# Attention and two layers of experts: the gates computed behind the first block and stored as lines, pieces of weights measured later, the last scatters unordered and in half rows

## The chip, the cores and the metric

The kernel runs on one core of one Trainium2 chip. The metric is the device time of one execution in microseconds (us). The core has TensorE (PE, multiplications into PSUM), VectorE (DVE), ScalarE (ACT), GpSimd (POOL, which also issues indirect DMAs) and SyncE (SP, which here issues most other DMAs), and 16 DMA engines between memory and SBUF.

## What is computed

Attention over 2 x 8 heads of 768 positions and 64 values, with a window of 16 and summaries of blocks of 32, gives 1,536 rows of 512 values. They pass through two layers of eight experts. In the first each row goes to the one expert with the largest logit; in the second each row goes to all experts, and their results are mixed.

```python
logits = x @ w_gate
expert_idx = np.argmax(logits, axis=1)
probs = softmax(logits)                                   # first layer
out[mask] = probs[arange, expert_idx][mask, None] * (relu(x[mask] @ w1[e]) @ w2[e])
...
P = np.exp(x @ w_gate - max)                              # second layer
for _ in range(8): P /= P.sum(1); P /= P.sum(0); P *= N / E
out += P[:, e:e + 1] * (relu(x @ w1[e]) @ w2[e])          # for all e
```

## The kernel before

The attention writes its result as columns into `xT`; `finished` makes the logits `lg` of two tiles of 128 rows; `rows_out` (L534) turns a tile back and stores it as rows in DRAM, `xd`. The copies `xn` that it stores from have three buffers. Routing (`experts`, `ranks`, `by_lane` and what follows, L379 to L672) sorts the rows by expert into blocks of 256 places: `row_i` says which row stands at a place, `seat_i` where its result goes. 100 filler multiplications (`warm`, L174) follow on PE.

The first layer of experts then runs block by block (`compute`). `fetch(n)` gathers the rows of block n from `xd` with two indirect DMAs on POOL (L1034), and loads its weights, eight pieces of 512 KB, through four buffers `kx` on SP's queue (L152 for w1, L958 for w2). Each piece is split by ACT (`wh`, L944) and DVE (`wl`, L946) into a high and a low part. `turn_rows` transposes the rows (L1066) and splits them (`xh` L1071, `xl` L1072). Layer 1 (L979) makes `hh` and `hl` of 8 column groups, layer 2 (L1001) the results `py`, which are squared, scaled and scattered to `yd` (L1114). For block 0 the w1 pieces are loaded ahead, on a guess of the expert; a branch that every engine takes (L1126, L1127) loads them again if the guess was wrong.

Beside the blocks stands other work, a list of steps called `more`. It is woven from lists with a start each, and one step of it is done at every other call of `step()` inside a block; blocks 1 to 5 take `each` steps apiece. In it are: `gate_square` and `gate_rate` (the size of the second layer's gate weights); `gates` (the exponential and sums that give the first layer's gate of each row), and `gates_out`, which stores them in DRAM, `gd`; and `plain(i, p)` for eight pieces of the second layer's first expert: load into one of three buffers `raw`, square and sum on ACT (`measure`, L740), a rate from it, then the high and low parts. Piece i starts at step 4 i, and piece i + 3 takes the same buffer. The code's order is not the last word: a scheduler places each instruction on its engine by its priorities and by when its operands can be there, and `tc.issue_after(x)` holds an instruction behind x. Thus `gate_square`, `gates` and `gates_out` stood far ahead of block 1, in the routing, since nothing held them there.

The gates are read back as `gated`, by an indirect gather on `gd` (L850), between the two layers.

The second layer takes the largest part of the time. It works by a plan of ticks (`at(tick, f)`), written out by hand: `first` and `second` are its two products, `mixing` gives the functions of the mixing weights, one per tick of a list. `acc` holds the results of all rows in SBUF. In `second`, for the last expert, DVE adds the last parts of two tiles of rows, h = 0 whole at i = 4 and h = 1 by halves at i = 5 (columns 256 on) and i = 6 (columns up to 256), in the order of `SECOND`, 0, 1, 3, 2, 5, 4, 6. Behind i = 4 and i = 6 the tile is scattered to `out` by an indirect DMA on POOL (L1486), twelve in all. All write the same tensor, so each waits for the one before it.

Of the kernel before, what the change touches and what calls it, by code (L numbers as in the profile page):

```python
# [23 lines left out]
P = 128  # L24
NT = B * S
# [83 lines left out]
def body(ctx: ExitStack, tc: tile.TileContext, q, k, v, wg1, w1a, w2a, wg2, w1b, w2b, cst, out):  # L109
# [26 lines left out]
    gex = const.tile([P, NTB, E], F32, name="gex")  # L136
    gse = const.tile([P, NTB], F32, name="gse")
    nblk_i = const.tile([1, 1], I32, name="nblk_i")
    eblk_i = const.tile([1, NBLK], I32, name="eblk_i")
# [878 lines left out]
    if True:  # L1018
# [117 lines left out]
        def gate_square():  # L1136
            sq = wq.tile([P, KC * E], F32, name="wgsq")
            nc.scalar.activation(sq, wg2_sb, AF.Square, accum_out=wgq)
            nc.gpsimd.tensor_copy(wgqb, wgq)
# [6 lines left out]
        def plain(i, p):  # L1146
            idle = lambda: None
            raw = raws[i % 3]
            junk = raw[:, 4:6].rearrange("p a f -> p (a f)").bitcast(BF16)
            return [lambda: p.load(raw), idle, idle, lambda: p.measure(junk), p.measured, p.rate, lambda: (p.raw_hi(), p.sums(fast=True)), lambda: (p.raw_lo(), p.sum4(fast=True)),  # L1150
                    idle, p.sum_hi, p.sum_lo]

        def gates():
            sh = [P, NTB, E]
            nc.vector.tensor_tensor(out=gex, in0=lg, in1=mx.unsqueeze(2).to_broadcast(sh), op=ALU.subtract)
            nc.scalar.activation(gex, gex, AF.Exp)
            nc.vector.tensor_reduce(out=gse, in_=gex, axis=AX.X, op=ALU.add)
            nc.vector.tensor_scalar(gse, gse, 1e-9, None, op0=ALU.add)
            nc.vector.reciprocal(gse, gse)
            nc.vector.tensor_tensor(out=gex, in0=gex, in1=oh, op=ALU.mult)  # L1160
            nc.vector.tensor_reduce(out=gate, in_=gex, axis=AX.X, op=ALU.add)
            nc.vector.tensor_tensor(out=gate, in0=gate, in1=gse, op=ALU.mult)

        def gates_out():
            nc.sync.dma_start(out=gd.rearrange("(t p) o -> p (t o)", p=P), in_=gate)

        more = weave(
            [(0, [gate_square, gate_rate]), (2, [gates, lambda: None, gates_out])]
            + [(4 * i, plain(i, p)) for i, p in enumerate(p2 + p1)]
            + [(4 * (2 * F2 - 1) + 6, [level])]  # L1170
        )
# [92 lines left out]
    def mixing():  # L1264
# [5 lines left out]
        def start1():  # L1270
# [5 lines left out]
            nc.vector.tensor_reduce(out=st[0], in_=lg2, axis=AX.XY, op=ALU.max)  # L1276

        def start2():
            pmt = pz.tile([1, P], F32, tag="m", name="pmt")
            nc.tensor.transpose(pmt, st[0], ident)  # L1280
            st.append(g2.tile([1, 1], F32, tag="gm", name="gm", bufs=1))
            nc.vector.tensor_reduce(out=st[1], in_=pmt, axis=AX.X, op=ALU.max, negate=True)
# [31 lines left out]

        return [start1, start2, start3] + [turn1, turn2, turn3] * 8 + [end]

# [118 lines left out]
    def second(e, k, s, i):  # L1435
# [45 lines left out]
        if i in (2, 4) or e == E - 1:  # L1481
            nc.vector.scalar_tensor_tensor(out=to, in0=p, scalar=w, in1=to, op0=ALU.mult, op1=ALU.add)  # L1482
            if i == 4 and e < E - 1:
                nc.gpsimd.dma_start(out=to, in_=gs[0], accum_op=ALU.add)  # L1484
            if e == E - 1 and i in (4, 6):
                nc.gpsimd.indirect_dma_start(  # L1486
                    out=out, out_offset=bass.IndirectOffsetOnAxis(ap=token_i[:, t : t + 1], axis=0), in_=acc[:, t], in_offset=None,
                    bounds_check=NT - 1, oob_is_err=True,
                )
            return  # L1490
        if i in (0, 5):
# [19 lines left out]
    turns = [66 + 6 * i + t for i in range(8) for t in (0, 2, 4)]  # L1511
    for tick, f in zip([55, 58, 62] + turns + [115], mix):
        at(tick, f)
# [110 lines left out]
```

## Time and profile before

| | us |
|---|---|
| median of 3 runs | 1250.6 |
| lowest and highest | 1245.0, 1256.08 |
| the profiled execution | 1249.01 |
| its span in the profile | 1247.2 |

Mean granted clock of PE over the span: 0.984 (1.00 is 2.4 GHz). Busy shares: PE 95%, DVE 78%, ACT 68%, POOL 21%. Times in the trace are counted from the span's start. A row of the timeline gives start, duration, engine, line, operation and tiles, the count of merged instructions, and in brackets how long its engine stood idle before it and what ended that. Lines are those of the kernel before.

### The profile page before, as it was taken

The numbers are of one execution on the slowest core, as the hardware profiler recorded it, in microseconds if no ns is written. First come the engines' busy times: TensorE is split into PE (matmuls) and PEld (weight loads), VectorE is DVE, ScalarE is ACT, GpSimd is POOL, SyncE is SP. The second block draws the span as 40 slices with busy tenths as digits, with TensorE's granted clock in tenths as the row PEclk, the third lists the DMA queues.
The fourth block names the chain that finished last, engine by engine and source line by source line (L and its number), as shares of the span: only waits on it lengthen the run. The fifth ranks groups of instructions, "written<-read, shape, count | busy, mean of one in ns | idle before, by whom it ended". The sixth has DMA issues, their size and how long they took to land. (4 is left out here: it accounts for less than half of the span.)

```text
span 1247.2 us, 27484 instructions
## 1 busy us (share of the span) xinstructions
PE 1181.1 (95%) x10473; PEld 1044.1 (84%) x10473; DVE 972.6 (78%) x1950; ACT 846.0 (68%) x1595; POOL 265.9 (21%) x331
## 2 busy tenths in 40 slices
PE   6898799999889999999999999999999999999997
PEld 5776688888778788888888888888888888888886
DVE  6695578884588898897878788788978878796763
ACT  5585467774677767776877677677767767776440
POOL 4351212312221220120121112111211211121011
PEclk9899799999999999999999999999999999999999
DMA  9947687862335543665556566555656655663201
GB/s 206 205 97 206 155 275 257 253 208 96 112 111 157 140 130 96 161 148 142 131 119 141 145 162 146 144 115 122 156 137 161 138 135 126 138 149 94 68 35 52
DMA packets 186496, 179.79 MB, mean 144 GB/s; under 512 B 35872, under 2 KB 159520, under 8 KB 185968
## 3 DMA queue, kind: packets, MB, share of 16 engines
q1 hardware_dynamic: 159648, 136.41, 38.6%
q0 software_dynamic: 26704, 41.50, 17.9%
q8 instruction: 85, 1.39, 0.5%
q14 instruction: 59, 0.48, 0.1%
HBM read 131.38 MB, written 15.53 MB: 118 GB/s over the span
## 5 line engine op out<-in xcount | busy, mean ns | idle before, releaser
L1365 PEld LDWEIGHTS <-w1h 128*128 128x128 f16 x2688 | 258.3, 98 | 46.0 <-issue 15.9
L1451 PEld LDWEIGHTS <-hh 128*128 128x128 f16 x2688 | 263.4, 98 | 32.0 <-issue 1.2
L1365 PE MATMUL fx<-kx,w1h 128*128 128x256 f16 x1472 | 257.3, 272 | 8.2 <-ACT c L1372 4.6
L1451 PE MATMUL gx<-w2l,hh 128*128 128x256 f16 x768 | 209.3, 273 | 1.1 <-DVE w2l L780 1.1
L1451 PE MATMUL gx<-w2h,hh 128*128 128x256 f16 x768 | 209.3, 273 | 1.0 <-DVE acc L1482 1.0
L1451 PE MATMUL gx<-w2h,hl 128*128 128x256 f16 x768 | 209.3, 273 | 0.0
L1365 PE MATMUL fx<-kx,w1l 128*128 128x256 f16 x736 | 200.5, 272 | 0.0
L1365 PE MATMUL fa<-kx,w1h 128*128 128x256 f16 x1104 | 193.7, 273 | 0.7 <-ACT yb L1113 0.7
L1372 ACT ACTIVATE c<-fx,kap 128x256 f32<-128x256 f32 x288 | 134.5, 473 | 79.3 <-PE fx L1365 78.8
L1451 PE MATMUL ga<-w2h,hh 128*128 128x256 f16 x576 | 157.6, 274 | 0.0
L1451 PE MATMUL ga<-w2l,hh 128*128 128x256 f16 x576 | 157.6, 274 | 0.0
L1451 PE MATMUL ga<-w2h,hl 128*128 128x256 f16 x576 | 157.5, 273 | 0.0
L1365 PE MATMUL fa<-kx,w1l 128*128 128x256 f16 x552 | 150.7, 273 | 0.0
L1365 PEld LDWEIGHTS <-w1l 128*128 128x128 f16 x1344 | 131.4, 98 | 17.2 <-issue 1.8
L1451 PEld LDWEIGHTS <-hl 128*128 128x128 f16 x1344 | 131.7, 98 | 16.7 <-issue 1.3
L1420 DVE TENSOR_TENSOR hl<-c,hh 128x1024 f16<-128x1024 f32 x96 | 117.1, 1220 | 26.4 <-ACT hh L1417 25.7
L1417 ACT CAST hh<-c 128x1024 f16<-128x1024 f32 x96 | 99.8, 1040 | 34.6 <-DVE c L1414 34.2
L1493 ACT ACTIVATE y<-gx,pws 128x256 f32<-128x256 f32 x144 | 68.2, 474 | 79.9 <-PE gx L1451 62.2
L753 POOL DMA_DIRECT2D raw<-raw x77 | 77.1, 1031 | 210.3 <-DVE w2l L780 97.4
L1375 DVE SCALAR_TENSOR_TENSOR c<-fa,kap,c 128x512 f32<-128x512 f32 x96 | 71.7, 747 | 46.3 <-PE fa L1365 39.9
L1408 DVE SCALAR_TENSOR_TENSOR hl<-c,hh 128x768 f16<-128x768 f32 x96 | 91.2, 950 | 15.4 <-ACT hh L1405 15.4
L1484 POOL DMA_DIRECT2D acc<-y x36 | 31.4, 871 | 336.8 <-ACT c L1372 265.9
(263 smaller groups left out, 2438.6 us busy)
## 6 DMA issues: line engine op xcount, KB each, us to landing
raw<-in_moe_w SPq DMA_DIRECT2D x228, 128.0 KB, 3.5
kx<-in_moe_w SPq DMA_DIRECT2D x56, 512.0 KB, 5.0
kx<-xohd SPq DMA_DIRECT2D x147, 128.0 KB, 3.3
kx<-xold SPq DMA_DIRECT2D x147, 128.0 KB, 3.1
acc<-y POOLq DMA_DIRECT2D x72, 256.0 KB, 4.5
raw<-raw POOLq DMA_DIRECT2D x77, 128.0 KB, 3.6
raw<-in_moe_w SPq DMA_DIRECT2D x38, 256.0 KB, 3.6
vt<-in_v SPq DMA_DIRECT2D x16, 240.0 KB, 7.5
```

Of the source, the lines that this page charges most:

```text
L753: nc.gpsimd.dma_start(out=self.raw[:, to], in_=self.raw[:, of], accum_op=ALU.add)
L1365: nc.tensor.matmul(p, l[:, a, kc * P : (kc + 1) * P], r[:, j, kc], start=new and kc == 0 and m == 0, stop=kc == K2 - 1 and m == 2, skip_gr ...
L1372: nc.scalar.activation(c[:, q], p, f, scale=k_)
L1375: nc.vector.scalar_tensor_tensor(out=c[:, q], in0=x, scalar=k_, in1=c[:, q], op0=ALU.mult, op1=ALU.add)
L1408: nc.vector.scalar_tensor_tensor(out=h[1][:, :3], in0=raw, scalar=0.0, in1=h[0][:, :3], op0=ALU.max, op1=ALU.subtract)
L1417: nc.scalar.copy(h[0][:, 3:], c)
L1420: nc.vector.tensor_tensor(out=h[1][:, 3:], in0=c, in1=h[0][:, 3:], op=ALU.subtract)
L1451: nc.tensor.matmul(p, l, r, start=new and f == 0 and m == 0, stop=f == F2 - 1 and m == 2, skip_group_check=True)
L1484: nc.gpsimd.dma_start(out=to, in_=gs[0], accum_op=ALU.add)
L1493: nc.scalar.activation(gs[h][:, d], p, AF.Copy, scale=w)
```

## The change

It has three parts. First, `gate_square` and `gates` are held behind the layer 1 that was issued last when they are called (`taken[-1]`, which is block 0's or block 1's), `gates` a step later in the list, and `gates_out` turns the gates by a transpose on PE into 12 lines of 128 values and stores those. Second, in `plain` two more idle steps stand between a piece's load and its measurement, and `level` moves by two; the list `more` grows from 39 to 41 steps, and `each` from 8 to 9. Third, for the last expert h = 1 of a pair of tiles is scattered in two half rows, behind i = 5 and i = 6, through a view of `out` with twice as many rows and indices `half_i`; and the scatters are declared free of order among each other.

```diff
+    gt = const.tile([NTB, P], F32, name="gt")
+    half_i = const.tile([P, HTB, 2], U32, name="half_i")
...
-            nc.scalar.activation(sq, wg2_sb, AF.Square, accum_out=wgq)
+            with tc.issue_after(taken[-1][0].ins):
+                nc.scalar.activation(sq, wg2_sb, AF.Square, accum_out=wgq)
...
-            return [lambda: p.load(raw), idle, idle, lambda: p.measure(junk), p.measured, p.rate, lambda: (p.raw_hi(), p.sums(fast=True)), lambda: (p.raw_lo(), p.sum4(fast=True)),
+            return [lambda: p.load(raw), idle, idle, idle, idle, lambda: p.measure(junk), p.measured, p.rate, lambda: (p.raw_hi(), p.sums(fast=True)), lambda: (p.raw_lo(), p.sum4(fast=True)),
                     idle, p.sum_hi, p.sum_lo]
...
-            nc.vector.tensor_tensor(out=gex, in0=lg, in1=mx.unsqueeze(2).to_broadcast(sh), op=ALU.subtract)
+            with tc.issue_after(taken[-1][1].ins):
+                nc.vector.tensor_tensor(out=gex, in0=lg, in1=mx.unsqueeze(2).to_broadcast(sh), op=ALU.subtract)
...
-            nc.sync.dma_start(out=gd.rearrange("(t p) o -> p (t o)", p=P), in_=gate)
+            pt = ps_m.tile([NTB, P], F32, tag="m", name="pt")
+            nc.tensor.transpose(pt, gate, ident)
+            nc.scalar.copy(gt, pt)
+            nc.sync.dma_start(out=gd.rearrange("(t p) o -> t (p o)", p=P), in_=gt)
...
-            [(0, [gate_square, gate_rate]), (2, [gates, lambda: None, gates_out])]
+            [(0, [gate_square, gate_rate]), (3, [gates, lambda: None, gates_out])]
             + [(4 * i, plain(i, p)) for i, p in enumerate(p2 + p1)]
-            + [(4 * (2 * F2 - 1) + 6, [level])]
+            + [(4 * (2 * F2 - 1) + 8, [level])]
...
+        def halves():
+            for h in range(2):
+                nc.vector.tensor_scalar(half_i[:, :, h], token_i[:, HTB:], 2, h, op0=ALU.mult, op1=ALU.add)
...
-            if e == E - 1 and i in (4, 6):
-                nc.gpsimd.indirect_dma_start(
-                    out=out, out_offset=bass.IndirectOffsetOnAxis(ap=token_i[:, t : t + 1], axis=0), in_=acc[:, t], in_offset=None,
-                    bounds_check=NT - 1, oob_is_err=True,
+            if e == E - 1 and i in (4, 5, 6):
+                if i == 4:
+                    to, at_, rows, n = out, token_i[:, t : t + 1], acc[:, t], NT
+                else:
+                    to, at_ = out.rearrange("t (h d) -> (t h) d", h=2), half_i[:, t - HTB, 6 - i : 7 - i]
+                    rows, n = acc[:, t, d], 2 * NT
+                put = nc.gpsimd.indirect_dma_start(
+                    out=to, out_offset=bass.IndirectOffsetOnAxis(ap=at_, axis=0), in_=rows, in_offset=None,
+                    bounds_check=n - 1, oob_is_err=True,
                 )
+                tc.declare_no_dep(put.ins, group="rows", reason="disjoint rows")
+                tc.add_to_no_dep_group("rows", put.ins)
...
-    for tick, f in zip([55, 58, 62] + turns + [115], mix):
+    for tick, f in zip([55, 58, 62] + turns + [115, 118], mix):
```

The order on SP, at the end of the routing, before the change (`raw` are pieces of the second layer, `xn` the rows, `gate` the gates, `eblk_i` the block's expert):

```order
L167 DMA raw_93<-in_moe_w 128x256
L534 DMA xd<-xn 128x512 x3
L1165 DMA gd<-gate 128x12x1
L534 DMA xd<-xn 128x512 x3
L1045 TENSOR_LOAD eblk_i
```

and of the change:

```order
L167 DMA raw_94<-in_moe_w 128x2x256
L168 DMA raw_94<-in_moe_w 128x256
L169 DMA raw_94<-in_moe_w 128x256
L167 DMA raw_95<-in_moe_w 128x2x256
L168 DMA raw_95<-in_moe_w 128x256
L169 DMA raw_95<-in_moe_w 128x256
L536 DMA xd<-xn 128x512 x6
L1047 TENSOR_LOAD eblk_i
```

The store of the gates has left its place between the third and the fourth store of rows; it now stands, as `gd<-gt 12x128`, among the loads of block 2's weights.

The order on ACT, from the routing's last copies to block 0's first relu, before the change (`wgsq` is `gate_square`, `raw,ssq` a measurement):

```order
L533 COPY xn<-pr 128x512 x2
L1156 ACTIVATE gex<-gex 128x96
L533 COPY xn<-pr 128x512 x4
L740 ACTIVATE raw_91,ssq_1730<-raw_91 128x1024
L1138 ACTIVATE wgsq,wgq<-wg_sb 128x32
L740 ACTIVATE raw_92,ssq_1730<-raw_92 128x1024
L740 ACTIVATE raw_93,ssq_1730<-raw_93 128x1024
L1126 TENSOR_LOAD eblk_i
L1127 COMPARE_AND_BRANCH
L1127 UNCONDITIONAL_BRANCH x2
L944 CAST wh_1763<-kx 128x1024
L944 CAST wh_1765<-kx 128x1024
```

and of the change:

```order
L535 COPY xn<-pr 128x512 x6
L742 ACTIVATE raw_93,ssq_1732<-raw_93 128x1024
L742 ACTIVATE raw_94,ssq_1732<-raw_94 128x1024
L742 ACTIVATE raw_95,ssq_1732<-raw_95 128x1024
L1128 TENSOR_LOAD eblk_i
L1129 COMPARE_AND_BRANCH
L1129 UNCONDITIONAL_BRANCH x2
L946 CAST wh_1765<-kx 128x1024
L946 CAST wh_1767<-kx 128x1024
```

`gate_square` and the gates' exponential have left this stretch; the first stands in block 0's layer 2 now, the second in block 1's layer 1.

The order on POOL at the kernel's end, with the semaphores that each waits for (DMASW are those of its own DMAs, one after another), before the change:

```order
L1486 DMA out<-acc,token_i 1536x512 [waits DMASW4_49,DVE_49]
L1486 DMA out<-acc,token_i 1536x512 [waits DMASW5_49,DMASW4_49,DVE_49]
L1486 DMA out<-acc,token_i 1536x512 [waits DMASW6_49,DMASW5_49,DVE_49]
L1486 DMA out<-acc,token_i 1536x512 [waits DMASW7_49,DMASW6_49,DVE_49]
L1486 DMA out<-acc,token_i 1536x512 [waits DMASW7_49,DMASW0_49,DVE_49]
```

and of the change:

```order
L1502 DMA out<-acc,half_i 3072x256 [waits DMASW4_49,DVE_49]
L1502 DMA out<-acc,token_i 1536x512 [waits DMASW5_49,DVE_49]
L1502 DMA out<-acc,half_i 3072x256 [waits DMASW6_49,DVE_49]
L1502 DMA out<-acc,half_i 3072x256 [waits DMASW7_49,DVE_49]
L1502 DMA out<-acc,token_i 1536x512 [waits DMASW0_49,DVE_49]
```

There are 18 scatters instead of 12, and the wait for the one just before is gone; a wait for the DMA that used the same semaphore eight DMAs earlier is left.

## Rows read from the trace of the kernel before

**Rows 1.** Windows: us, busy per engine (instructions), PE's granted clock, DMA share, GB/s.

```profile
118.00:150.00 32.00, 20.36 (x191) 18.16 (x190) 17.78 (x64) 12.54 (x24) 8.02 (x10) 0.73 0.75 148
...
400.00:1200.00 800.00, 791.96 (x7267) 706.98 (x7265) 659.02 (x1286) 577.02 (x989) 145.25 (x170) 1.00 0.55 132
```

**Rows 2.** Timeline of PE, 112 to 165 us.

```profile
121.88 0.66 PE L531 MATMUL pr<-ident,xT 128*128 128x128 f32 x4 [0.52 <-ACT xn L533]
...
125.31 7.55 PE L174 MATMUL warm<-ones_b 128*128 128x128 bf16 x100
...
139.71 1.76 PE L1066 MATMUL pt<-ident,xb 128*128 128x128 f32 x7 [0.74 <-DMA xb<-xd,row_i]
...
144.58 0.58 PE L979 MATMUL ph<-xl,wh 128*128 128x256 f32 x1 [1.25 <-DVE xl L1072]
```

**Rows 3.** Timeline of POOL, 100 to 180 us.

```profile
134.82 1.17 POOL L1034 DMA_INDIRECT xb<-xd,row_i  x1 [8.89 <-DMA xd<-xn]
136.30 1.05 POOL L1034 DMA_INDIRECT xb<-xd,row_i  x1 [0.30 <-issue]
```

**Rows 4.** DMA issues, 119.2 to 119.9 us; the last figure is us to landing.

```profile
xd<-xn SPq DMA_DIRECT2D x1, 256.0 KB, 2.0
```

**Rows 5.** DMA, 122.2 to 123 us.

```profile
DMA packets 1251, 0.03 MB, mean 42 GB/s; under 512 B 1244, under 2 KB 1244, under 8 KB 1250
...
xd<-xn SPq DMA_DIRECT2D x2, 256.0 KB, 11.0
```

**Rows 6.** DMA issues, 125.5 to 127 us.

```profile
xd<-xn SPq DMA_DIRECT2D x1, 256.0 KB, 8.1
```

**Rows 7.** Timeline of SP's queue, 100 to 180 us.

```profile
121.05 0.37 SPq L1165 DMA_DIRECT2D gd<-gate  x1
121.85 4.20 SPq L534 DMA_DIRECT2D xd<-xn  x3
```

**Rows 8.** Timeline of ACT, 112 to 165 us.

```profile
119.52 0.28 ACT L1156 ACTIVATE gex<-gex 128x96 f32<-128x96 f32 x1
...
125.12 0.59 ACT L533 COPY xn<-pr 128x512 f32<-128x512 f32 x1 [2.75 <-DMA xd<-xn]
127.33 1.06 ACT L740 ACTIVATE raw<-raw 128x1024 bf16<-128x1024 f32 x1 [1.63 <-DVE seat_i L672]
...
137.50 0.23 ACT L1138 ACTIVATE wgsq<-wg_sb 128x32 f32<-128x32 f32 x1 [9.02 <-POOL wgq L1043]
...
139.81 1.98 ACT L944 CAST wh<-kx 128x1024 fp32r<-128x1024 f32 x2
```

**Rows 9.** Timeline of DVE, 112 to 165 us.

```profile
120.24 0.26 DVE L1160 TENSOR_TENSOR gex<-gex,oh 128x96 f32<-128x96 f32 x1
...
141.56 2.37 DVE L946 TENSOR_TENSOR wl<-kx,wh 128x1024 fp32r<-128x1024 f32 x2
```

**Rows 10.** Windows of layer 1 alone (L979): PE, weight loads, clock, DMA.

```profile
145.00:149.00 4.00, 4.00 (x20) 4.00 (x20) 0.50 0.95 314
151.00:155.00 4.00, 4.00 (x35) 4.00 (x35) 1.00 0.51 166
```

**Rows 11.** Timeline of ACT, 215 to 305 us.

```profile
249.80 1.06 ACT L740 ACTIVATE raw<-raw 128x1024 bf16<-128x1024 f32 x1 [2.77 <-DMA raw<-in_moe_w]
```

**Rows 12.** Timeline of PE, 250 to 265 us.

```profile
252.33 0.39 PE L979 MATMUL ph<-xh,wh 128*128 128x256 f32 x1 [1.54 <-DVE hl L985]
```

**Rows 13.** Waits of SP's queue, 160 to 300 us: total, times, longest.

```profile
SPq L733 <- DVE w2l L780: 7.0, 5, 3.1
```

**Rows 14.** Timeline of POOL, 1200 us to the end.

```profile
1237.89 0.98 POOL L1486 DMA_INDIRECT out<-acc,token_i  x1 [4.68 <-DVE acc L1482]
1241.36 0.98 POOL L1486 DMA_INDIRECT out<-acc,token_i  x1 [2.49 <-DMA out<-acc,token_i]
```

**Rows 15.** DMA issues, 1200 us to the end.

```profile
out<-acc,token_i POOLq DMA_INDIRECT x8, 2.7
```

**Rows 16.** Timeline of DVE, 1200 us to the end.

```profile
1238.17 0.48 DVE L1482 SCALAR_TENSOR_TENSOR acc<-gx,pws,acc 128x256 f32<-128x256 f32 x1 [0.56 <-PE gx L1451]
```

More of the change, by code (lines that the diff above doesn't have):

```diff
@@ L1313, in end @@
             weigh(0)
-        return [start1, start2, start3] + [turn1, turn2, turn3] * 8 + [end]
+        return [start1, start2, start3] + [turn1, turn2, turn3] * 8 + [end, halves]
     def weigh(e):
```

## The prediction

> **What bounds the kernel now.** I first split the span into stretches [rows 1]. From 400 to 1200 us TensorE (PE) is busy for 791.96 of 800 us: the second layer of experts is bound by multiplications, of which the change moves none. From 118 to 150 us it is busy for 20.36 of 32 us and its granted clock averages 0.73. That is the passage from routing to the first block of the first experts, and there a few microseconds can be had without less work. The other place is the end, where PE has finished and scatters still leave one by one.
>
> The passage, followed back from its result. Layer 1 of block 0 gets into its stride at 144.58, when the low half of the rows (`xl`) is there [rows 2]. The gather that fetches these rows starts on POOL at 134.82, after 8.89 us in which it waited for the stores `xd<-xn` [rows 3]. So I looked at the stores. One issued at 119.2 to 119.9 lands 2.0 us later [rows 4]; those issued at 122.2 to 123 take 11.0 us [rows 5]; the last takes 8.1 us and lands at about 133.8 [rows 6]. What lies between is the store of the gates, issued at 121.05 [rows 7]: 128 partitions of 12 single values, that is 1,536 pieces of 4 bytes. In 0.8 us, 1,251 packets passed, 1,244 of them under 512 B, and they carried 0.03 MB [rows 5]. The transfers after them are the slow ones. The Trainium skill, "DMA: Bandwidth & Descriptors", Specifications, asks for at least 512 B in a transfer and says that a shorter one is read, modified and written. By that rule 12 lines of 512 B are not in the slow class, and the trace agrees as far as it can: the slowness begins with the short packets.
>
> **The change, part by part.**
>
> The store of the gates leaves the queue between the rows' stores. Now six row stores follow each other. The sixth copy `xn` waited 2.75 us on ACT for the third store [rows 8]; its transposes end at 121.88 + 0.66 = 122.5 [rows 2], so its copy (0.59) ends at 123.2 and its store goes out at 123.3. At the 2.0 us of rows 4 it lands at 125.3; I take 125.6. The gather then starts about a microsecond later, as it does now (133.8 to 134.82): 126.6. The second starts 1.5 us after it, at 128.1 (134.82 to 136.30 [rows 3]), and its rows reach PE 3.4 us on (136.30 to 139.71 [rows 2]): 131.5. That is 8.2 us earlier, but other things are now late. PE is in its 100 filler multiplications until 125.31 + 7.55 = 132.9 [rows 2]. And ACT: today it stands 9.02 us at `gate_square`, which waits for a memset behind the gathers, with two measurements and the casts `wh` queued behind it [rows 8]. In the changed order `gate_square` stands after block 0's casts, so the three measurements run from 127.33 on, at 1.06 each and some 0.2 for reading the sum: to 131.1. With half a microsecond for the branch, the casts start at 131.5 (now 139.81). Today PE resumes 4.8 us after the casts begin; DVE's first `wl` begins 0.8 us after the first of the two casts ends (139.81 + 0.99 to 141.56 [rows 9]), since DVE is still summing pieces; those sums can now run under the measurements, which saves some 0.7. So PE resumes at 135.6 instead of 144.58: 9.0 us. Bounds: 7.0, if the last store lands 2 us later than the chain has room for, and 9.2.
>
> The clock. In 145 to 149 the granted clock is 0.50 (1.2 GHz) and 20 multiplications of layer 1 start in 4 us; in 151 to 155 it is 1.00 and 35 do [rows 10]. It fell after PE had had nothing since 132.9. In the changed kernel PE goes from fillers to transposes to layer 1, with about 1 us of holes. If the clock holds, what now takes 144.58 to 149.9, some 26 multiplications, takes 26/8.75 = 3.0 instead of 5.3 us: 2.3 us. Bounds 0 and 2.3. Layer 2 and block 1 follow, since the loads of weights are released by the same chain: `w2` loads by the first `wl`, block 1's by casts tied to layer 1.
>
> Pieces measured two steps later. At 249.80 ACT waited 2.77 us for a piece's load before it could square it [rows 11], and the relu of layer 1 was queued behind; PE stood 1.54 us at 252.33 [rows 12]. Two more steps between load and measurement cover that: 1.5 us. Against it: a raw buffer is now given back in the very step that loads it again, and SP stands at such loads already (7.0 us in 5 waits, at most 3.1 [rows 13]), with the blocks' own weights queued behind. I take no loss in the sum. Bounds: 1.5 gained to 1.5 lost.
>
> The gates behind block 0. Eight short DVE instructions (the longest 0.26 [rows 9]) and an exponential of 0.28 on ACT [rows 8] leave the routing and shorten at_tile's chain by some 0.1, which the fillers hide. In block 1 they come back, 8 x 0.2 = 1.6 us on DVE, covered by multiplications of layer 2. Not covered: the new transpose of `gate` stands in PE's order after 13 products of layer 2, some 3.0 us in (13 x 0.23, twice the 4/35 of rows 10 for twice the columns), and waits for a DVE chain that I put at 3.4 after layer 2's start (last `hl` some 0.9, four of the gates' instructions 1.0, one `wl` 1.2 as in rows 9, the last product 0.2, semaphores 0.1): +0.4 us. Bounds 0 and 1.5, the latter if that `wl` waits for its load.
>
> The end. The scatter that ends the kernel starts at 1241.36 because it waited for the one before it to land (2.49 us of idle before it, landing 2.7 [rows 14, 15]). Its data were ready at 1238.17 + 0.48 = 1238.65 [rows 16]. Without the order, POOL can start it when the scatter issued at 1237.89 has been generated, 0.98 later, plus 0.3 between two of them (as between 134.82 + 1.17 and 136.30 [rows 3]): 1239.2. That is 2.2 us earlier. The additional half scatter at i = 5 is generated at about 1236.3, and is out of the way by 1237.3. Bounds 1.2 (if POOL needs a second one in between) and 2.5 (a half row lands sooner). The Trainium skill, "DMA: Bandwidth & Descriptors", Anatomy of one DMA, fits 2.0 us + bytes/436 GB/s; for 256 KB that is 2.6, near the 2.7 here, and for the half 2.3. By it the end would come 0.3 earlier still. The two instructions of `halves` lie at tick 118 on a DVE that has idle time there: nothing.
>
> Sum: -9.0 - 2.3 - 1.5 + 0.4 - 2.2 = -14.6 us on the profiled execution's 1249.0 us: 1234.4. That execution is 1.6 below the median shown (1250.6), so a median would be 1236.0; I say 1235. About 1% (12.5 us) is what a measurement of this kernel can tell from no change.
>
> **Rivals.**
>
> The short packets cost only themselves. Then the rows' stores are late for a reason of their own, and the first wait shrinks by the packets' own 1.3 us or so. For: they pass quickly, 1,251 in 0.8 us. Against: the store just ahead lands in 2.0. The terms are then -1.3, no clock, -1.5, +0.4, -2.2: -4.6, or 1245 to 1246. The Trainium skill, the same page, Measured, has about 10.5 ns a packet; by that alone the 1,536 packets on 16 engines would be 1.0 us, this rival's side. That the trace's slow packets come after them speaks against it.
>
> Given back in blocks 1 to 5. Every load after block 0 starts earlier, yet the pieces bunch: nine steps a block instead of eight put two loads of pieces in block 2 where there was one. If the blocks' casts then wait for weights and the low clock also stays, 4 to 8 us of the 14.6 go: 1239 to 1243.
>
> Slower. SP's order is the place: five pieces are loaded again behind the give-back. Each would have to hold SP, and with it the block's weights, for more than 2.9 us in full view of PE before 5 x 2.9 = 14.6 is eaten; at 5 us each, 25 - 14.6 = +10, or 1260. Speaks for it: single waits of 3.1 us exist. Against: PE shows none of them today, and the changed order puts weights ahead of the pieces' loads.
>
> **How the numbers follow.** Forecast, 1230 to 1239: 0.65. Given back: 0.18. Short packets cost only themselves: 0.10. Slower: 0.03. The rest, 0.04, is more than forecast, below 1230 (block 1's waits go too). Faster by over 1% means below 1238: nine tenths of the forecast, all of the rest, a little of the second rival, 0.64. Slower by over 1%: 0.03. Within: 0.33. The range, with 1 in 10 left out above (most of the short-packet case and the slower one) and as much below: 1229 to 1244; the forecast's own is 1230 to 1239.
>
> **What would show it.** In the new profile: the last `xd<-xn` lands within 3.5 us; the first gather starts at 126 to 128; PE has no hole over 1.5 us between fillers and layer 1, and a granted clock of 1.00 there; layer 1 of block 0 in its stride at 135 to 137. ACT's waits for `raw` loads are gone, and PE's waits for `hl` in blocks 1 to 5 lack the 1.54 us of rows 12 and have no new one of that size. The transpose of `gate` waits under 1 us. The last scatter starts 0.6 us after the last DVE instruction. Wrong I would be if stores still land late without the short packets, or if SP's waits at the pieces' loads show up as PE's waits for weights.

## The result and the profile after the change

| | before | changed |
|---|---|---|
| median, us | 1249.46 (4 runs) | 1232.59 (4 runs) |
| lowest and highest | 1245.0, 1256.08 | 1231.74, 1234.73 |
| ratio to before, 95% interval | | 0.9863 (0.9816 to 0.991) |
| span of the profiled execution | 1247.2 | 1231.1 |

The median fell by 16.9 us, 14.6 had been forecast, from 1249.0 for the profiled execution. Between the profiled executions it is 16.1.

The two traces can be laid on one another at four points: the product that gives the rows' numbers (`prow`, the last of the routing on PE), the first product of layer 2 in block 0, the first of the last layer 2, and the end of the last DVE instruction. `prow` itself starts between 121.8 and 125.6 us in the executions told of here, whatever the kernel, so that each stretch is counted from it. "Passage" is `prow` to layer 2 of block 0, "blocks" from there to the last layer 2, "second layer" from there to the last DVE instruction, and "end" from there to the end of the span.

| stretch, us | before | changed | difference | forecast |
|---|---|---|---|---|
| start to `prow` | 124.99 | 123.81 | -1.18 | 0 |
| passage | 33.16 | 22.30 | -10.86 | -9.0 - 2.3 = -11.3 |
| blocks | 151.25 | 151.24 | -0.01 | -1.5 + 0.4 = -1.1 |
| second layer | 929.25 | 929.26 | +0.01 | 0 |
| end | 8.55 | 4.49 | -4.06 | -2.2 |

The whole stretch of the passage, against [rows 1]:

```profile
118.00:150.00 32.00, 27.14 (x269) 25.24 (x268) 24.81 (x67) 19.84 (x33) 6.77 (x8) 0.95 0.60 199
...
400.00:1200.00 800.00, 791.01 (x7258) 706.24 (x7256) 658.53 (x1282) 571.22 (x977) 147.97 (x172) 1.00 0.55 130
```

PE works for 27.14 of 32 us instead of 20.36, at a granted clock of 0.95 instead of 0.73. The second layer is untouched. DMA issues between 118 and 130 us, against [rows 4 to 6]:

```profile
xd<-xn SPq DMA_DIRECT2D x6, 256.0 KB, 2.0
xb<-xd,row_i POOLq DMA_INDIRECT x3, 3.5
```

Six stores of rows, 2.0 us to landing in the median; the third takes 4.1, none takes 8 or 11. POOL, ACT and PE, against [rows 3, 8, 2]:

```profile
126.74 1.17 POOL L1036 DMA_INDIRECT xb<-xd,row_i  x1 [1.96 <-DMA xd<-xn]
```

```profile
123.27 0.58 ACT L535 COPY xn<-pr 128x512 f32<-128x512 f32 x1 [1.98 <-DMA xd<-xn]
126.15 1.06 ACT L742 ACTIVATE raw<-raw 128x1024 bf16<-128x1024 f32 x1 [2.30 <-DVE seat_i L674]
...
130.70 2.00 ACT L946 CAST wh<-kx 128x1024 fp32r<-128x1024 f32 x2 [1.31 <-SPq L1129]
```

```profile
123.81 0.49 PE L653 MATMUL prow<-at_tile,at_lane 128*128 128x26 f16 x12 [2.64 <-DVE at_tile L630]
124.15 7.21 PE L176 MATMUL warm<-ones_b 128*128 128x128 bf16 x100
...
134.85 0.38 PE L981 MATMUL ph<-xl,wh 128*128 128x256 f32 x1 [1.01 <-DVE xl L1074]
...
178.23 0.27 PE L1170 MATMUL pt<-ident,gate 128*12 128x128 f32 x1 [0.61 <-DVE gate L1166]
```

The gather starts 2.93 us behind `prow` instead of 9.83, and layer 1 gets into its stride 11.04 behind it instead of 19.59. Layer 1 by stretches, against [rows 10] (PE, weight loads, clock, DMA):

```profile
141.00:145.00 4.00, 4.00 (x35) 4.00 (x35) 1.00 0.79 259
160.00:164.00 4.00, 3.25 (x18) 3.04 (x17) 0.67 0.82 256
```

In block 0 the clock is whole, 35 products in 4 us instead of 20. In block 1 it is 0.67 between 160 and 164 (before, it was 1.00 in block 1): a part of the gain that is given back. For all of PE it is 0.82, 0.50 and 0.83 in the three stretches of 2 us from 160.1; the shares that are missing, times 2 us each, make some 1.7 us, an estimate that is used again below for other falls of the clock.

The end: POOL and DVE (against [rows 14, 16]), and DMA issues from 1226.5 us (against [rows 15]).

```profile
1225.85 0.98 POOL L1502 DMA_INDIRECT out<-acc,token_i  x1 [0.60 <-DVE acc L1493]
1227.13 0.98 POOL L1502 DMA_INDIRECT out<-acc,half_i  x1 [0.30 <-issue]
```

```profile
1226.13 0.48 DVE L1493 SCALAR_TENSOR_TENSOR acc<-gx,pws,acc 128x256 f32<-128x256 f32 x1 [0.56 <-PE gx L1462]
```

```profile
out<-acc,half_i POOLq DMA_INDIRECT x1, 2.4
```

The last scatter starts 0.52 us after the last DVE instruction's end (2.71 before) and lands 2.4 us later (2.7 before). From its landing to the span's end 1.57 us pass (1227.13 + 2.4 = 1229.53 to 1231.1), where before there were 3.15 (1241.36 + 2.69 to 1247.2).

### The profile page after: what moved, and what is told of

It reads as the page before. It is cut to its first block, busy times and chain, and to the rows that moved or that the text cites. A ratio compares the mean times of both kernels' runs of the same rounds, so it can differ in the third digit from the quotient of the medians.

```text
span 1231.1 us, 27502 instructions
## 1 busy us (share of the span) xinstructions
PE 1176.5 (96%) x10474; PEld 1040.6 (85%) x10474; DVE 972.2 (79%) x1952; ACT 845.4 (69%) x1596; POOL 272.0 (22%) x337
## 4 chain that ended last, share of the span: by engine, by line
PE 62%; issue 12%; DVE 6%; DMA 4%; ACT 3%; POOL 2%; SPq 0%; POOLq 0%; ACTq 0%; DVEq 0%
PE fx L1376 15%; PE gx L1462 15%; PE fa L1376 11%; PE ga L1462 11%; PE py L1003 5%; PE ph L981 4%; DMA kx<-in_moe_w 2%; POOL out L1502 1%; DMA acc<-y 1%; DVE wl L948 1%; ACT wh L946 1%; DVE c L1386 1%; ACT raw L742 0%; DVE hl L1419 0%; ACT c L1383 0%
## 5 line engine op out<-in xcount | busy, mean ns | idle before, releaser
L1376 PE MATMUL fa<-kx,w1l 128*128 128x256 f16 x552 | 150.7, 273 | 0.0
```

What stands on the lines that cost most here:

```text
L1376: nc.tensor.matmul(p, l[:, a, kc * P : (kc + 1) * P], r[:, j, kc], start=new and kc == 0 and m == 0, stop=kc == K2 - 1 and m == 2, skip_gr ...
```

## The experiments

Twelve kernels ran. Their stretches, in us:

| run | median | passage | blocks | second layer | end |
|---|---|---|---|---|---|
| before | 1249.5 | 33.16 | 151.25 | 929.25 | 8.55 |
| changed | 1232.6 | 22.30 | 151.24 | 929.26 | 4.49 |
| e1 pieces added | 1240.1 | 30.10 | 150.69 | 928.37 | 4.57 |
| e2 pieces 512 B apart | 1235.0 | 22.33 | 153.23 | 931.09 | 4.52 |
| e9 pieces 64 B apart | 1233.3 | 25.91 | 149.89 | 928.18 | 4.51 |
| e3 lines, else as before | 1241.2 | 24.23 | 155.84 | 927.98 | 8.58 |
| e4 changed, measured early | 1236.7 | 23.02 | 156.62 | 928.64 | 4.54 |
| e5 before, measured late | 1248.7 | 32.26 | 154.05 | 928.95 | 8.52 |
| e6 whole rows, no order | 1235.0 | 22.23 | 153.20 | 930.37 | 6.39 |
| e7 half rows, ordered | 1240.9 | 22.04 | 151.55 | 929.48 | 10.90 |
| e8 pieces at the new place | 1241.5 | 22.16 | 159.13 | 927.89 | 4.54 |
| v1 rows early | 1231.9 | 24.84 | 147.53 | 930.66 | 4.51 |
| v2 branch early | 1233.3 | 21.98 | 152.33 | 927.28 | 4.54 |
| v3 both | 1228.3 | 21.51 | 148.16 | 929.47 | 4.59 |

The medians were taken in five sets, each with runs of the kernel before beside it (their medians 1248.7 to 1249.6). The stretches are of one execution each. Among the changed kernel and those that differ from it only in the passage's stores or at the end (e1, e2, e6, e7, e9), the blocks spread from 149.9 to 153.2, so a difference below some 3 us in that column says nothing. The granted clock accounts for most of that spread: it does not fall in the blocks of e1 and e9 (150.7 and 149.9), falls for some 1.7 us in the changed kernel and e7 (151.2 and 151.6), and for some 3.4 in e2 and e6 (153.2 both).

### Is it the short pieces?

**e1** puts a store of 1,536 values, which nobody reads, back between the rows' stores of the changed kernel.

```diff
+    gd2 = dram.tile([NT, 1], F32, name="gd2")
...
+        nc.sync.dma_start(out=gd2[:, 0:1].rearrange("(t p) o -> p (t o)", p=P), in_=rank)
```

> The changed kernel with one store added and nothing taken away: 1,536 single values of 4 bytes (the ranks, which nobody reads) go to a tensor of their own, from the place on SP at which the gates' store stood, between the third and the fourth store of rows. Theory 1, the short pieces make the transfers behind them slow: the stores of rows behind it land 8 to 11 us after issue instead of 2, the first gather starts at 133 to 135 instead of 126.7, layer 1 of block 0 gets into its stride 7 to 9 us later than 134.85, part of it at the low clock, and the time is 1241 to 1244. Theory 2, the pieces cost only their own passage of about 1 us: gather at 127.5 to 128, time 1233 to 1234.

**e2** and **e9** spread the same values.

```diff
-    gd2 = dram.tile([NT, 1], F32, name="gd2")
+    gd2 = dram.tile([NT, 128], F32, name="gd2")
```

In e9 the 128 is 16.

> The same added store of 1,536 pieces of 4 bytes, but each piece goes to a line of 512 bytes of its own. If the shortness of the pieces is what makes the following transfers slow, this is as slow as the run with the pieces side by side: 1241 to 1244, gather at 133 to 135. If it is that pieces of many partitions are written into the same few lines of memory, the following stores land in 2 to 4 us, the gather starts at 127 to 129 and the time is 1233 to 1235.

> Again the changed kernel with a store of 1,536 single values of 4 bytes added between the third and the fourth store of rows, now each 64 bytes from the next. Side by side they held up the next stores (first gather 13.5 us behind the last transposes of rows, against 6.2 without them); 512 bytes apart they did not (7.1). If writes into the same 64 bytes are what holds them up, the gather starts 7 to 7.5 us behind those transposes, 1233 to 1235. If it takes neighbours within a longer stretch than 64 bytes, something between: 9 to 13.5 us, 1236 to 1241.

The first gather on POOL and `prow` on PE, of e1, then e2, then e9:

```profile
135.50 1.34 POOL L1038 DMA_INDIRECT xb<-xd,row_i  x1 [9.27 <-DMA xd<-xn]
```

```profile
125.27 0.50 PE L655 MATMUL prow<-at_tile,at_lane 128*128 128x26 f16 x12 [2.64 <-DVE at_tile L631]
```

```profile
128.92 1.26 POOL L1038 DMA_INDIRECT xb<-xd,row_i  x1 [2.82 <-DMA xd<-xn]
```

```profile
125.13 0.50 PE L655 MATMUL prow<-at_tile,at_lane 128*128 128x26 f16 x12 [2.64 <-DVE at_tile L631]
```

```profile
127.71 1.17 POOL L1038 DMA_INDIRECT xb<-xd,row_i  x1 [2.93 <-DMA xd<-xn]
```

```profile
123.81 0.50 PE L655 MATMUL prow<-at_tile,at_lane 128*128 128x26 f16 x12 [2.63 <-DVE at_tile L631]
```

The last copy of rows on ACT, from which the last store goes out, again of e1, e2 and e9:

```profile
123.41 0.59 ACT L536 COPY xn<-pr 128x512 f32<-128x512 f32 x1 [0.68 <-DMA xd<-xn]
```

```profile
125.36 0.58 ACT L536 COPY xn<-pr 128x512 f32<-128x512 f32 x1 [2.78 <-DMA xd<-xn]
```

```profile
124.15 0.59 ACT L536 COPY xn<-pr 128x512 f32<-128x512 f32 x1 [2.87 <-DMA xd<-xn]
```

Side by side, the values bring back the wait whole: the gather comes 10.23 us behind `prow` (before the change 9.83), and the passage is 7.8 longer than the changed kernel's. That is theory 1; the time, 1240.1, is a little under its range. With the same number of pieces of the same 4 bytes, but 512 or 64 bytes from each other, the gather comes 3.79 and 3.90 behind `prow`, 0.9 and 1.0 later than without them (2.93). Even that lies ahead of the last store: its copy waits 2.78 and 2.87 us for the third store, which had gone out before the pieces, and this wait varies without pieces too (1.98 in the changed kernel, 2.35 in v2, 0.65 in e4). From the end of that copy to the gather there are 2.98 and 2.97 us, against 2.89 in the changed kernel and 11.50 in e1. So the shortness isn't what holds up the stores behind; that the values lie side by side, 16 of them to each 64 bytes, is. Which distance between 4 and 64 bytes is enough, and whether it is the shared 64 bytes or the 6 KB that all the values share (96 KB in e9), no run shows, and how the chip works that off, the trace does not show either. (The passage of e9 is 3.6 longer than the changed kernel's, though its gather is not: there PE's fillers have pauses for which the trace names no wait, and the granted clock is 0.50 from 134 to 138 us, after them.)

**e8** stores single values side by side at the new place, among the loads of weights, instead of the 12 lines.

```diff
-            pt = ps_m.tile([NTB, P], F32, tag="m", name="pt")
-            nc.tensor.transpose(pt, gate, ident)
-            nc.scalar.copy(gt, pt)
-            nc.sync.dma_start(out=gd.rearrange("(t p) o -> t (p o)", p=P), in_=gt)
+            nc.sync.dma_start(out=gd.rearrange("(t p) o -> p (t o)", p=P), in_=gate)
```

> The changed kernel, but the gates are stored as 1,536 single values again, at the new place (among the loads of block 2's weights). The prediction put no cost on the store's new place. Theory 1, the pieces hold up whatever is behind them on the queues, wherever they stand: the loads of weights issued behind the store land 8 to 11 us later than now, ACT or DVE waits for one and PE gets a hole of some us in block 1 or 2: 1236 to 1240. Theory 2, a load is wanted only some 8 us after it is issued there, so most of the delay is covered: 1233 to 1234. Theory 3, only writes are held up, not loads: 1232.6.

DMA issues from 180 to 195 us, e8 and then the changed kernel:

```profile
kx<-in_moe_w SPq DMA_DIRECT2D x4, 512.0 KB, 12.3
raw<-in_moe_w SPq DMA_DIRECT2D x1, 128.0 KB, 9.2
xb<-xd,row_i POOLq DMA_INDIRECT x2, 12.6
```

```profile
kx<-in_moe_w SPq DMA_DIRECT2D x4, 512.0 KB, 4.5
...
xb<-xd,row_i POOLq DMA_INDIRECT x2, 4.0
```

Theory 1, and more: loads are held up like stores, and POOL's gathers like SP's transfers. The blocks take 159.13 us, the median is 8.9 us above the changed kernel's. Of the 7.9 us more in the blocks, 3.2 are a pause of PE for which the trace names no wait (it stands in four other kernels too, see the last section). Passage and blocks together take 181.3 us in e8, 173.5 in the changed kernel and 184.4 before: moved behind the passage without the 12 lines, the store would have left some 3 us of the gain of 10.9.

### Is the store all of it?

**e3** is the kernel before with the 12 lines alone, which also takes the store out of the passage.

```diff
+    gt = const.tile([NTB, P], F32, name="gt")
...
-            nc.sync.dma_start(out=gd.rearrange("(t p) o -> p (t o)", p=P), in_=gate)
+            pt = ps_m.tile([NTB, P], F32, tag="m", name="pt")
+            nc.tensor.transpose(pt, gate, ident)
+            nc.scalar.copy(gt, pt)
+            nc.sync.dma_start(out=gd.rearrange("(t p) o -> t (p o)", p=P), in_=gt)
```

> The kernel before with the gates' store alone changed: transposed on PE and stored as 12 lines. The gates themselves, gate_square and everything else stay where they were, the pieces are measured as before, the scatters are in order. The store goes out in block 1, so nothing stands between the stores of rows. Theory 1 (the store of pieces is the cause, the holds of gate_square and the gates matter little): stores land in 2 us, gather at 127 to 128, gate_square waits on ACT only 2 to 3 us instead of 9.02, layer 1 in stride at 136 to 138, clock 1.00 there, time 1239 to 1242 against 1249.5. Rival (holding gate_square carries the gain, since ACT stands behind it): layer 1 starts no earlier than 141, time 1244 to 1249.

ACT in e3:

```profile
129.75 0.23 ACT L1139 ACTIVATE wgsq<-wg_sb 128x32 f32<-128x32 f32 x1 [2.39 <-POOL wgq L1044]
...
132.06 1.98 ACT L945 CAST wh<-kx 128x1024 fp32r<-128x1024 f32 x2
```

Theory 1. The passage is 8.9 us shorter than before, and `gate_square` stands 2.39 us instead of 9.02. The casts begin 8.19 behind `prow` (123.87), in the changed kernel 6.89: holding `gate_square` and the gates back is worth the rest, 1.2 to 1.9 us of passage (e4, which holds them and measures early as e3 does, has 23.02). But the blocks take 155.84 instead of 151.25: about half of what the passage gained is given back there. Some 3.4 us of that, by the estimate above, are two falls of the clock, which did not fall in the blocks before; PE's waits in the blocks grew from 7.2 to 8.6.

### What is measuring later worth?

**e4** takes the two idle steps from the changed kernel, **e5** puts them alone into the kernel before.

```diff
-            return [lambda: p.load(raw), idle, idle, idle, idle, lambda: p.measure(junk), ...
+            return [lambda: p.load(raw), idle, idle, lambda: p.measure(junk), ...
...
-            + [(4 * (2 * F2 - 1) + 8, [level])]
+            + [(4 * (2 * F2 - 1) + 6, [level])]
```

> The changed kernel without its second part: the pieces are measured two steps earlier, as before. As predicted (two steps more cover a wait of ACT): 1.5 us slower than the changed kernel, 1234. Rival (the wait only moved, ACT's waits for raw loads were 6.0 us in 3 after the change against 3.7 in 2 before): the same within 1 us, 1232 to 1233; or faster by up to 1.5, 1231.

> The kernel before with the second part of the change alone: pieces measured two steps later, nothing else. As predicted, a term of its own: PE's wait of 1.54 us at 252.33 goes, 1248.0 against 1249.5. Rival 1, it is worth more, because the two kernels with and without it lie 5.4 us apart between layer 2 of block 0 and the last layer 2 (151.2 against 156.6): 1244 to 1246. Rival 2, it is worth something only when the blocks start early, since the late start hides the waits: 1249.5, no difference.

PE's waits between layer 2 of block 0 and the last layer 2, e4 (144 to 302 us) and the changed kernel (146 to 298):

```profile
PE ph L981 <- DVE hl L987: 3.6, 3, 1.9
PE ph L981 <- issue: 2.7, 1, 2.7
PE ph L981 <- DVE xl L1074: 1.8, 2, 1.0
```

```profile
PE ph L981 <- DVE hl L987: 1.9, 2, 1.1
PE ph L981 <- DVE xl L1074: 1.7, 2, 1.0
PE pt L1068 <- DVE gsc L683: 1.3, 1, 1.3
PE pt L1170 <- DVE gate L1166: 0.6, 1, 0.6
```

ACT's waits for pieces from 140 to 300 us, before and changed:

```profile
ACT raw L740 <- DMA raw<-in_moe_w: 3.7, 2, 2.8
```

```profile
ACT raw L742 <- DMA raw<-in_moe_w: 6.0, 3, 2.7
```

PE's waits from 155 to 309 us in e5, against 3.3 us for `hl` and none for `gsc` before the change, and then two us of e4 behind PE's pause, with columns as in [rows 1] (the granted clock is 0.50):

```profile
PE pt L1066 <- DVE gsc L681: 1.9, 1, 1.9
...
PE ph L979 <- DVE hl L985: 1.0, 2, 0.6
```

```profile
288.80:290.80 2.00, 2.00 (x12) 2.00 (x11) 0.10 (x1) 0.38 (x1) 0.19 (x1) 0.50 0.42 147
```

Alone, in the kernel before, it is worth nothing (ratio 0.9991, 0.9973 to 1.0009). Taken from the changed kernel, it costs 4.1 us in the median, more than e4's expectations had, with blocks of 156.6 us, as in e3 (155.8), which measures early too. By the times that is rival 2 of e5; that the measuring is the reason is not shown. Of the 5.4 us by which e4's blocks are longer, 2.7 are one pause of PE, which ends at 287.76 and for which the trace names no wait, and some 1.7 (the estimate above) the clock, which falls right behind it. e5 measures late and has both as well, a pause of 2.8 us and the fall behind it; the kernel before has the pause (2.6) without the fall.

What the two steps do can be read from PE's waits. Those for `hl` become shorter, 1.0 us in e5 instead of 3.3 before, and 1.9 in the changed kernel instead of 3.6 in e4. In their place the transposes of a later block's rows wait 1.9 and 1.3 us for `gsc`, which belongs to the rate of a piece; none of the kernels that measure early has this wait. ACT's waits for pieces did not become less: 6.0 us in the changed kernel and 4.8 in e4, 7.0 in e5 and 3.7 before.

### What made the end shorter?

**e6** keeps the order free, but scatters whole rows; **e7** keeps the half rows, but in order.

```diff
-            if e == E - 1 and i in (4, 5, 6):
-                if i == 4:
+            if e == E - 1 and i in (4, 6):
+                if True:
```

```diff
-                tc.declare_no_dep(put.ins, group="rows", reason="disjoint rows")
-                tc.add_to_no_dep_group("rows", put.ins)
```

> The changed kernel with the last scatters free of order, but h = 1 in whole rows behind i = 6, as before. Theory 1, the end gained by the order alone, and the half rows bring only the 0.3 us of a shorter landing: from the last DVE instruction to the span's end 4.8 to 5.0 us instead of 4.49, time 1233. Theory 2, the 1.6 us that the changed kernel is quicker behind its last landing come from the half rows: 6.0 to 6.5 us, time 1234 to 1235.

> The changed kernel with the half rows, but every scatter waits again for the one before it to land. Three scatters to a pair of tiles instead of two, each some 3.0 to 3.4 us: the last starts at about 3.5 us behind its data instead of 0.5, from the last DVE instruction to the span's end 8 us instead of 4.49, time 1236. If the end behind the last landing is short because the last scatter is a half one, it is 1.6 us behind the landing here too; if it is short because no order is there, 3.1 us.

The last scatters on POOL and the span, of e6 and then of e7:

```profile
1230.83 0.98 POOL L1502 DMA_INDIRECT out<-acc,token_i  x1 [0.31 <-issue]
```

```profile
core 0: 1236.7 us, clock 0.985
```

```profile
1232.10 0.98 POOL L1502 DMA_INDIRECT out<-acc,token_i  x1 [2.21 <-DMA out<-acc,half_i]
1235.64 0.98 POOL L1502 DMA_INDIRECT out<-acc,half_i  x1 [2.55 <-DMA out<-acc,token_i]
```

```profile
core 0: 1239.6 us, clock 0.985
```

From the last scatter's start to the span's end there are 5.84 us before the change (whole, ordered), 5.87 in e6 (whole, free), 3.96 in e7 (half, ordered) and 3.97 in the changed kernel (half, free). That goes by the size of the last scatter alone, theory 2 of e6. The order sets when it starts: 0.52 us behind its data in e6, 6.94 in e7. The 3.5 us expected for e7 was too little: three scatters, one after another, take 3.2 to 3.5 us each, some 9.9 for a pair of tiles, and the next pair comes 9.17 us later, so that the delay adds up over the last pairs. Half rows without the freedom would have made the end 2.4 us longer than before (10.90 against 8.55).

### What bounds the passage now?

**v1** takes three things out of the changed kernel's passage, **v2** another, **v3** all of them (with 82 fillers). First v1, then v2.

```diff
-            xn = a3.tile([P, DM], F32, tag="xn", name="xn")
+            xn = a3.tile([P, DM], F32, tag="xn", name="xn", bufs=6)
...
-        warm(ps_s, "s", 100, last.ins)
+        warm(ps_s, "s", 75, last.ins)
...
-            nc.scalar.activation(junk, raw, AF.Square, accum_out=ssq[self.x][:, self.i : self.i + 1])
+            with tc.issue_after(taken[0][0].ins) if taken else ExitStack():
+                nc.scalar.activation(junk, raw, AF.Square, accum_out=ssq[self.x][:, self.i : self.i + 1])
```

```diff
-                got["e"] = nc.sync.value_load(eblk_i[0:1, n : n + 1], min_val=0, max_val=E - 1)
+                with tc.issue_after(first_w2[0].ins) if 0 < n <= NMIN else ExitStack():
+                    got["e"] = nc.sync.value_load(eblk_i[0:1, n : n + 1], min_val=0, max_val=E - 1)
```

(`first_w2` holds the loads of w2, of which the first is block 0's.)

> The changed kernel with what its trace shows as the next bounds of the passage taken away: six buffers xn instead of three (ACT waited 1.98 us for a store before the last copy), the three measurements held behind block 0's first relu (casts stood behind them until 130.70), and 75 fillers instead of 100 (they ended at 131.4). Theory, the passage is still the bound: gather 1.5 to 2 us earlier, layer 1 of block 0 in stride at 132 to 133 instead of 134.85, time 1230 to 1231. Rival, blocks 1 to 5 are bound by loads or give it back through the low clock: 1232 to 1234.

> The changed kernel with one thing moved: SP's loads of the later blocks' expert numbers, which stood before SP's part of the branch (its load of block 0's number at 125.8, its branch only at 130.3), are held behind the loads of block 0's w2. Theory, ACT's casts wait for SP at the branch (1.31 us before 130.70): SP's branch at 126.5 to 127, casts right behind the three measurements at 129.4, xh 1 us earlier, stride of layer 1 about 1 us earlier than 134.85, as far as fillers (till 131.4) let it: time 1231.5 to 1232.5. Rival, nothing moves, since PE's fillers and DVE's sums are later anyway: 1232.6.

> The same with the other bounds taken away too: six buffers xn, measurements behind block 0's first relu, 82 fillers. In the run with these alone the casts began at 132.22, behind the branch, and the transposed rows waited for them, PE had holes of 1.44 and 0.94 us and a low clock for 6.8 us. Theory, with the branch early the casts are done before the rows come, layer 1 in stride 2.5 to 3 us earlier measured from the product that gives the rows' numbers (8.0 to 8.5 us behind it instead of 11.04), no low clock behind it: 1228.5 to 1230. Rival, blocks 1 to 5 are bound by the loads of weights and give it back: 1231.5 to 1233.

SP's loads of expert numbers in the changed kernel, and the first casts and rows on ACT in v1 and in v3:

```profile
L1047 SPq TENSOR_LOAD <-eblk_i x7: 262/262/754, 124.6 to 129.2; - x7
```

```profile
132.22 1.99 ACT L947 CAST wh<-kx 128x1024 fp32r<-128x1024 f32 x2 [9.83 <-DMA xb<-xd,row_i]
```

```profile
126.32 1.99 ACT L948 CAST wh<-kx 128x1024 fp32r<-128x1024 f32 x2 [6.43 <-SPq L1133]
131.68 1.07 ACT L1077 CAST xh<-pt 128x512 fp32r<-128x512 f32 x2 [3.36 <-PE pt L1072]
```

Layer 1 in v1 and in v3:

```profile
137.00:141.00 4.00, 4.00 (x21) 4.00 (x21) 0.50 0.90 332
```

```profile
134.00:138.00 4.00, 4.00 (x36) 4.00 (x35) 1.00 0.92 301
```

v1's gather comes 2.07 us behind `prow` instead of 2.93, but its casts wait, and PE stands 1.44 and 0.94 us before layer 1, which then runs at half the clock: the passage is 2.5 us longer. Even so v1 is no slower (0.9846, 0.9821 to 0.9872; 1231.9 lies between its theory and its rival), since its blocks take 147.5. v2 has no gain, its rival: fillers and sums are later anyway. In v3 both go together: the casts are done before the rows come, the clock is whole, passage 21.5, blocks 148.2, and 1228.27 us in the median (0.9824, 0.98 to 0.9848), 5.0 below v2 in the same set. Expected was a stride 8.0 to 8.5 us behind `prow`; it came 10.17 behind, since the 82 fillers took 7.42 us, as long as the 100 of the changed kernel (7.21), at a lower granted clock (0.51 and 0.64 from 122 to 130 us, against 0.73 and 0.84). That blocks shrink in v1 and v3 was not expected. In both the clock does not fall in the blocks, and PE's waits there are 3.5 and 4.3 us in sum, against 5.7 in the changed kernel; in v2 it does not fall either, but the waits are 7.1 and the blocks 152.3. Both hold the three measurements behind block 0's first relu, and both have six buffers and fewer fillers; no run has one of these alone, so which of them does it stayed open.

## Why the prediction was right, step by step

**The store of the gates, -9.0.** Its place in the argument was right: the late stores come from the transfer of single values, and without it layer 1 is 8.55 us earlier against `prow` (19.59 to 11.04). The 0.4 that are missing lie in ACT's casts, which came 6.89 behind `prow` where 6.5 had been forecast (131.5 against 124.99). Two terms in this were off and nearly cancelled: the three measurements ended 5.6 behind `prow` (at 129.38), not 6.1 (131.1), and for the branch, put at 0.5 us from no row, 1.31 passed.

The gather was to start 1.6 us behind `prow` (126.6 against 124.99) and came 2.93 behind: the prediction let the sixth copy `xn` follow its transposes, but with three buffers it still waits 1.98 us for the third store. This cost nothing, since the fillers and ACT's casts ended later. The step behind it is a misreading: "the store just ahead lands in 2.0" is [rows 4], the second store. The third, directly ahead of the gates' store (issued at about 120.3), took 4.7 us, and its counterpart in the changed kernel, with no short pieces on the queue, takes 4.1. So this store was slow mostly for another reason, and the pieces' share are the 8 and 11 us of those behind them.

What the prediction said on the reason is not right as it stands. It leaned on [rows 5] and on the Trainium skill, "DMA: Bandwidth & Descriptors", Specifications, which asks for at least 512 B for the full rate and has shorter transfers read, modified and written. Runs e2 and e9 send the same short transfers without the delay. What the runs show is narrower: short writes that lie side by side, 16 to each 64 bytes. The Trainium skill, the same page, Measured, has some 10.5 ns a packet, for loads that POOL issues; from it comes an estimate of 1.0 us for the 1,536 packets over 16 engines. The trace of e2 agrees for their passing (1,436 packets under 512 B between 123 and 124 us), and so does that of e1 (1,402 in the same microsecond): the pieces pass as quickly where they hold up the stores as where they don't. The rival "the short packets cost only themselves" is thus what pieces apart from each other do, and it was wrong for these, which lie side by side.

**The clock, -2.3.** As forecast: from the stride of layer 1 to layer 2 of block 0, 13.57 us before and 11.26 after, 2.31 less.

**Measured two steps later, -1.5.** The blocks' sum was forecast at -1.1 and measured 0.0, and the mechanism was wrong. The step that failed is to count a wait that goes as time gained, on the trace of before, without asking what PE meets in its place. PE's 1.54 us of [rows 12] are gone, and its waits for `hl` in the blocks fell from 3.3 to 1.9 us. But a wait of 1.3 for `gsc` came, and the clock falls in block 1 for some 1.7 (an estimate). ACT's waits for pieces, which should have gone, grew from 3.7 to 6.0 us. That the sum is 0.0 all the same is luck: the pause of 2.6 us without a named wait that PE has in the last block before the change is missing in the changed kernel's trace, and no run shows that the change took it away. In the kernel before the part is worth nothing (e5), and what it is worth beside the others stays open (e4).

The rival "given back in blocks 1 to 5" was right in part, with 4 to 8 us, casts that wait for weights and a low clock. e3, with the store alone, gives back 4.6 us in the blocks; ACT's casts wait 10.7 us for weights there instead of 5.8 (9.8 in the changed kernel), and the clock falls twice. Against the kernel before, though, the changed kernel gives back nothing in its sum.

**The gates' transpose, +0.4.** PE waited 0.61 us for `gate`.

**The end, -2.2.** The start of the last scatter moved by 2.19 us against its data, as worked out. The 1.9 us beyond it were not seen: 0.3 for a shorter landing, which the prediction told of beside its sum, and 1.6 between landing and the span's end. The prediction left that stretch as it was, and e6 and e7 show that it goes by the size of the last scatter.

**Slower, through SP's reloads**: no sign of it. By the stretches, -11.3 - 1.1 - 2.2 = -14.6 was forecast and -10.86 - 0.0 - 4.06 = -14.9 came, beside 1.2 us by which this execution reached `prow` earlier. That the two sums lie so near is luck in part: 1.9 us at the end that nobody had foreseen stand against 0.4 missing in the passage and 1.1 in the blocks.

## What to carry to other kernels

A small store can be dear for what stands behind it: look at the landing times of the transfers that follow it, and store such values as lines (a transpose on PE) or 64 bytes apart (in e9 nobody reads them, so what reading them back from there costs is not shown). When an early stage is made quicker, cost the parts that come after it again on the new start: waits move to another place, and a clock that is whole now may fall and give a part of the gain back. At the very end, look also at the stretch behind the last landing: a smaller last scatter shortened it by 1.6 us, but smaller scatters in order lengthened the end.

## What was not expected of the hardware

- 1,536 writes of 4 bytes side by side, 16 of them to each 64 bytes, hold up transfers of both SP and POOL, loads like stores, for some 8 to 10 us: 512 KB loads took 12.3 us instead of 4.5, gathers 12.6 instead of 4.0 (e8). 64 bytes apart, the same writes moved the gather by 0.1 us, counted from the last copy of rows (2.97 against 2.89), and by 1.0 counted from `prow`.
- From the start of the last scatter to the end of the span there are 5.8 to 5.9 us when it writes 256 KB, and 4.0 when it writes 128 KB; the landing accounts for 0.3 of this.
- In the last block of layer 1 PE pauses for 2.6 us in the kernel before, "issue" with no wait in the trace; in e3, e4, e5 and e8 for 2.6 to 3.2, in the changed kernel and the others for 0.9 or less. What sets this stayed open. In e4 and e5 the granted clock falls right behind the pause, to 0.50. In all five the pause begins within 0.5 us of a transfer on the DMA queue that the profile calls "instruction" (q8; at 295.0 to 295.5 in the kernel before, where the pause is 294.97 to 297.58), and two or one on another such queue (q14) come some 2 us later. That PE waits for its next instructions there is thus a guess with something for it, but it is not shown: the changed kernel has the same transfers (from 284 and 286 us on) without a pause.
